# Fourier mixing spread over all four head pairs of a batch, with a third pair of row buffers, and work of the hand-over moved into the first MLP tile

## The chip, the cores and the metric

One core of a Trainium2 chip runs the whole program. The metric is the device time of one execution in microseconds, the median of the runs shown. The engines are named as the profile names them: PE (matmul), DVE (vector), ACT (scalar), POOL (GpSimd) and SP, whose queue issues most DMAs.

## The reference

Causal attention with a forgetting bias, then a block that mixes tokens and channels by a two-dimensional Fourier transform, then a layer norm and an MLP, with a residual. B is 8, H is 8, S is 576, D is 64; the MLP goes 512 to 2048 to 512. All in float32.

```python
cum = cumsum(maximum(s, 0), -1)
scores = q @ k.T / sqrt(D) + minimum(-(cum[:, None] - cum[None, :]), 0)   # causal
attn = softmax(scores);  x = (attn @ v) as (B, S, H * D)
u = x + real(fft(fft(x, axis=1), axis=2))
un = (u - mean(u)) / sqrt(var(u) + 1e-6)
out = u + maximum(un @ w_ch1, 0) @ w_ch2
```

## The kernel before, in words

**Head pairs.** The loop over `i` goes through 32 pairs of heads, four to a batch (pair `i` is head pair `j = i % 4` of batch `b = i // 4`). One pass weaves generators ("streams") of several pairs: `scores(i)` (matmuls L491 and L492 into the PSUM tile ps, exponential L495 on ACT into P), `av(i - 1)` (matmuls L523), `maxes(i + 1)` (matmuls L459 into pm, row maxima L462 and L466 on DVE into Mx, transposed by L471), the splitting of q and k into high and low parts (`high`, `low`: L418, L420 on ACT, L435 on DVE, L438 on POOL), `recip(i - 2)` (the softmax denominators: sums, L538 and L539 on DVE, then by DMA through rd to the broadcast rb) and `finish(i - 2)` (L559: the pair's rows of x into xa, or by way of xr and three DMAs into xs). `weave` always takes the next step of the stream that has the smallest share of its total behind it. A stream is given as a generator and a total; a larger total makes it slower.

**Order.** PE's instructions stand in the order in which the Python code traces them, up to the MLP (`manual_schedule`). On the other engines, on all DMA queues, and in the MLP also on PE, the scheduler of the tile framework orders instructions at build time by its own model of time; the order is fixed in the program.

**Mixing.** When a batch is complete, `folds(b)` turns its xa and xs (two tiles of 128 x 2 x 576 floats each) into even and odd sums: per half jj an addition Aw on DVE (L251) and a subtraction Bw on POOL (L253), then Df and the split into De (L256, L70), then Df and the split into Do (L260, L70), and at the end the row e and its parts eh (L263 to L266). A split is a rounding copy on ACT (L69) and a subtraction on DVE (L70). `fourier(b)` then runs two passes. The first has three sine pieces (six matmuls L284 into pzs) and three cosine pieces (seven matmuls L292, L294 into pzc), each split into zs or zc. The second has, for two column halves kc, nine matmuls L306 into pyc and nine L315 into pys, each in three slices, then ym and yp (L320, L321 on DVE), four additions into xa and xs on POOL (L322 to L325), and at the end the write of xa and xs to uD in DRAM. Every fourth batch ends with a matmul group L336 and L338, L339. ps, pyc, pys, pzs, pzc and the MLP's h share three PSUM banks (`bank`); pm and pav share five others.

`folds(b)` begins in pair 4b + 6, and `fourier(b)` is traced in pairs 4b + 8 on. How much of it each pair takes, and at which pace, is in the table `MIX`, by `i % 4`; the whole costs FOURIER (8900) in the units in which its steps yield.

**Weights.** The MLP's weights come as 64 bit floats and are made into float32 on the chip, in chunks of 256 columns: L83, ACT's L84, L85, L88, L87, then POOL's L89. `convert_w` does 24 chunks and writes them to wD in DRAM; `load_w` reads those back for feed-forward blocks f below 6 and does the other 40 chunks itself (`rounded` in it), and splits all into wh and wl (L112, L114).

**The hand-over.** In pair 31 the first token tile's layer norm begins (`ln_tile`: mean, then the centred uch and ucl, then the squares' sum, var, and r, the reciprocal root, L158 and L159). Then one weave finishes `av(31)`, batch 6's mixing, the norm and the first weights, `finish(31)` and the folds of batch 7 follow, and nine MLP tiles of 512 tokens begin (`mlp_tile`: sixteen blocks f of twelve matmuls L183 into h, zh on ACT L187, zl on DVE L188, twelve matmuls L196 to L198 into acc). Batch 7's mixing is woven into the first MLP tile; weights from f = 8 on are loaded into space that the mixing's tiles leave.

## Time and profile before

| what | value |
|---|---|
| median of 3 runs | 1428.15 us (1423.54 to 1430.72) |
| the profiled execution | 1426.1 us, span 1424.4 us |
| PE busy | 1305.1 us (92%) |
| DVE busy | 745.7 us (52%) |
| POOL, ACT busy | 561.6 us (39%), 539.3 us (38%) |
| granted TensorE clock, mean | 0.971 |

All times within the kernel are microseconds from the start of the span. A group or wait that is named by a line (L466) is that line of the code above. In a wait, the name behind the arrow is what came last. Matmuls overlap, so the time of one row is a latency; what a sequence costs is read from start to start. The head pairs last until 544 us, the first MLP matmul starts at 572.4 us, and the first MLP tile ends at about 697.6 us.

### The profile page before, as it was taken

What the parts mean: (1) busy time and instruction counts of PE and PEld (TensorE: products, weight loads), DVE (VectorE), ACT (ScalarE), POOL (GpSimd) and SP (SyncE); (2) the same over time, 40 slices, a digit from 0 to 9 for tenths busy, and PEclk for the clock granted to TensorE, in tenths of its full rate; (3) what the DMA queues carried; (4) which work ended last, traced back from release to release, by engine and by line L of the source; (5) the groups of instructions that cost most, each with busy time, mean ns of one, the idle gap of its engine ahead of it and who ended that gap; (6) DMA issues with size and microseconds to landing.
All of it is one profiled execution on the core that took longest, in us unless ns stands there. A gap on an engine that the chain in (4) does not pass through costs nothing.

```text
span 1424.4 us, 17997 instructions
## 1 busy us (share of the span) xinstructions
PE 1305.1 (92%) x6190; PEld 1068.7 (75%) x6190; DVE 745.7 (52%) x1684; ACT 539.3 (38%) x1211; POOL 561.6 (39%) x543
## 2 busy tenths in 40 slices
PE   4887979897988887997899999999999999999998
PEld 3766868686777676775688888888888888888886
DVE  6667677877777788799833233222332223322212
ACT  4775756676665656344321121211212112121110
POOL 6445465656546566565720402204022040123300
PEclk9998999999999997999899999999999999999999
DMA  8555556565655555433200000000000000000000
GB/s 214 156 159 144 163 149 180 158 168 159 159 161 144 166 149 163 162 123 121 79 8 30 31 30 15 15 30 31 30 15 15 30 30 30 15 16 0 30 0 30
DMA packets 78230, 125.05 MB, mean 88 GB/s; under 512 B 11256, under 2 KB 36249, under 8 KB 78139
## 3 DMA queue, kind: packets, MB, share of 16 engines
q1 hardware_dynamic: 75627, 119.83, 28.4%
q0 software_dynamic: 1696, 2.50, 0.9%
q10 hardware_dynamic: 816, 1.57, 0.3%
q8 instruction: 49, 0.80, 0.2%
q14 instruction: 42, 0.34, 0.1%
HBM read 76.85 MB, written 23.07 MB: 70 GB/s over the span
## 4 chain that ended last, share of the span: by engine, by line
PE 51%; DVE 7%; POOL 2%; DMA 1%; issue 1%; ACT 1%; SPq 0%; DVEq 0%; POOLq 0%; ACTq 0%
PE h L183 25%; PE acc L198 8%; PE acc L196 8%; PE acc L197 8%; POOL we L89 1%; DVE wm L88 1%; DVE we L83 1%; DVE wm L85 1%; DVE we L87 1%; DVE wl L114 1%; ACT wh L112 1%; DMA wl<-wD 0%; POOL wl L114 0%; DVE ucl L148 0%; DVE zl L188 0%
## 5 line engine op out<-in xcount | busy, mean ns | idle before, releaser
L188 DVE SCALAR_TENSOR_TENSOR zl<-h,zh 128x512 fp32r<-128x512 f32 x144 | 98.6, 686 | 405.5 <-ACT zh L187 405.4
L187 ACT ACTIVATE zh<-h 128x512 fp32r<-128x512 f32 x144 | 85.9, 596 | 530.1 <-PE h L183 530.1
L198 PE MATMUL acc<-zl,wh 128*128 128x512 f32 x576 | 227.5, 396 | 4.9 <-DVE zl L188 4.9
L196 PE MATMUL acc<-zh,wh 128*128 128x512 f32 x576 | 227.6, 395 | 1.0 <-ACT zh L187 1.0
L197 PE MATMUL acc<-zh,wl 128*128 128x512 f32 x576 | 226.8, 394 | 0.0
L523 PE MATMUL pavB<-P,va 128*128 128x320 f32 (+2 forms) x640 | 189.1, 389 | 9.5 <-ACT stage L527 8.9
L459 PE MATMUL pm<-KQ 128*128 128x256 f32 (+3 forms) x384 | 156.5, 427 | 44.4 <-DVE Mx L466 23.1
L495 ACT ACTIVATE P<-ps 128x320 f32<-128x320 f32 (+4 forms) x384 | 145.9, 393 | 110.5 <-PE ps L492 106.8
L491 PE MATMUL ps<-KQ 128*128 128x256 f32 (+2 forms) x384 | 154.1, 404 | 24.4 <-ACT P L495 14.0
L183 PE MATMUL h<-uch,wh 128*128 128x512 f32 x576 | 159.9, 398 | 8.3 <-ACT wh L112 8.3
L183 PE MATMUL h<-uch,wl 128*128 128x512 f32 x576 | 158.1, 396 | 0.8 <-DVE wl L114 0.8
L183 PE MATMUL h<-ucl,wh 128*128 128x512 f32 x576 | 156.9, 393 | 0.0
L466 DVE CUSTOM_DVE_ANT_0 trash<-pm,amask 128x128 bf16<-128x128 f32 (+3 forms) x256 | 123.5, 482 | 34.2 <-PE pm L459 16.9
L212 POOL TENSOR_TENSOR o<-o,w 128x512 f32<-128x512 f32 x32 | 41.8, 1305 | 252.3 <-issue 218.5
L183 PEld LDWEIGHTS h<-uch,wh 128*128 128x128 f32 x576 | 108.2, 190 | 35.9 <-ACT wh L112 12.1
L198 PEld LDWEIGHTS acc<-zl,wh 128*128 128x128 f32 x576 | 108.7, 189 | 32.0 <-DVE zl L188 6.9
L183 PEld LDWEIGHTS h<-uch,wl 128*128 128x128 f32 x576 | 109.2, 190 | 26.6 <-DVE wl L114 1.2
L196 PEld LDWEIGHTS acc<-zh,wh 128*128 128x128 f32 x576 | 108.6, 188 | 26.1 <-ACT zh L187 1.8
L183 PEld LDWEIGHTS h<-ucl,wh 128*128 128x128 f32 x576 | 108.9, 189 | 24.7
L197 PEld LDWEIGHTS acc<-zh,wl 128*128 128x128 f32 x576 | 108.6, 189 | 24.7
L459 PEld LDWEIGHTS pm<-KQ 128*128 128x128 f32 x384 | 78.4, 207 | 64.7 <-DVE Mx L466 30.2
L492 PE MATMUL ps<-q,k 128*128 128x256 f32 (+2 forms) x384 | 120.5, 316 | 3.1 <-POOL q L438 3.1
(140 smaller groups left out, 2066.9 us busy)
## 6 DMA issues: line engine op xcount, KB each, us to landing
qk<-in_qkT_dram SPq DMA_DIRECT2D x32, 576.0 KB
raw<-in_wP_dram SPq DMA_DIRECT2D x64, 256.0 KB
va<-in_vA_dram SPq DMA_DIRECT2D x32, 480.0 KB
q<-KQ SPq DMA_DIRECT2D x32, 288.0 KB
k<-KQ SPq DMA_DIRECT2D x32, 288.0 KB
rb<-rd SPq DMA_DIRECT2D x64, 144.0 KB
u<-uD SPq DMA_DIRECT2D x8, 1024.0 KB
out_dram<-o SPq DMA_DIRECT2D x32, 256.0 KB
```

Source lines behind the costliest of these rows:

```text
L183: nc.tensor.matmul(h[:, :n], a[:, j * 128:(j + 1) * 128], b[:, j, :n], start=i == 0, stop=i == 11)
L187: nc.scalar.activation(zh[:, :n], h[:, :n], AF.Relu)
L188: nc.vector.scalar_tensor_tensor(out=zl[:, :n], in0=h[:, :n], scalar=0.0, in1=zh[:, :n].bitcast(F32), op0=ALU.max, op1=ALU.subtract)
L196: nc.tensor.matmul(acc[j][:, :n], a[:, cs], y[:, :n], start=g == 0, stop=False)
L197: nc.tensor.matmul(acc[j][:, :n], b[:, cs], y[:, :n], start=False, stop=False)
L198: nc.tensor.matmul(acc[j][:, :n], a[:, cs], z[:, :n], start=False, stop=g == NF - 1)
L459: nc.tensor.matmul(p[:, :n], qy[:, h, 128 * c:128 * c + 128], ky[:, h, k0:k0 + n], start=True, stop=True)
L466: nc.vector.tensor_tensor_reduce(out=trash[:nq, :n], in0=p[:nq, :n], in1=amask[:nq, m0:m0 + n], scale=1.0, scalar=first if x else NEG, op0 ...
L491: nc.tensor.matmul(p[:, :n], ky[:, h, ksl], qy[:, h, a:a + n], start=True, stop=False)
L492: nc.tensor.matmul(p[:, :n], k1[:, h, ksl], q1[:, h, a:a + n], start=False, stop=True)
L495: nc.scalar.activation(P[:, o:o + a + n - lo], p[:, lo - a:n], AF.Exp, scale=0.125)
L523: nc.tensor.matmul(p[:, a - lo:n], va[:, c, vs], P[:, o:o + w], start=c == 0, stop=c == cs[-1])
```

## The change

`MIX` gives each of the four head pairs about a quarter of a batch's mixing (0.22, 0.26, 0.26 and the rest), where the first two had 0.3 each and the third took the rest. As mixing then reaches into the fourth pair, xa and xs get three buffers instead of two; the space comes from the descriptor area for POOL's DMAs, cut to 4096 bytes of a partition. The copy of row xs[0, 0] to x256 moves from the end of `folds` to the start of `fourier`. The folds are traced three steps in the third pair and four in the fourth, where it was five and two. The share of `convert_w` is 1.5 times as large in pairs 0 and 1 and half as large in pairs 2 and 3.

In the hand-over, batch 6's mixing stops after 4500 units, its first pass; its second pass and all of batch 7's mixing follow in the weave of the first MLP tile, and so does the rest of the first tile's norm (the squares' sum, var and r). For that, `ln_tile` allocates r and fills LN after its fourth centred block.

```diff
-    MIX = ((0.3, 0.25), (0.3, 0.4), (1, 0.35), (1, 0.05))
+    MIX = ((0.22, 0.22), (0.26, 0.26), (0.26, 0.26), (1, 0.26))
...
-            xbuf[b] = (fft.tile([128, 2, S], F32, tag="xa", name="xa", bufs=2), fft.tile([128, 2, S], F32, tag="xs", name="xs", bufs=2))
+            xbuf[b] = (fft.tile([128, 2, S], F32, tag="xa", name="xa", bufs=3), fft.tile([128, 2, S], F32, tag="xs", name="xs", bufs=3))
...
-            streams.append([later(take(folding, 5), 2), 7 / 0.7])
+            streams.append([later(take(folding, 3), 3), 6])
...
-            streams.append([folding, FOLDS - 5])
+            streams.append([folding, (FOLDS - 3) / 0.8])
...
-        share = NC1 * 4.0 / (NP - 2) if i < NP - 2 else (1.0, 4.0)[i - NP]
+        share = NC1 * 4.0 / (NP - 2) * (1.5, 1.5, 0.5, 0.5)[i % 4] if i < NP - 2 else (1.0, 4.0)[i - NP]
...
-    weave([later(call(recip, NP - 2), 2), 10], [later(call(finish, NP - 2), 4), 10], [av(NP - 1), AV], [mixing, FOURIER * 0.1], [norm, 6 * 0.4],
+    weave([later(call(recip, NP - 2), 2), 10], [later(call(finish, NP - 2), 4), 10], [av(NP - 1), AV], [take(mixing, 4500), FOURIER * 0.1],
...
-    mixing = fourier(b, *xbuf.pop(b))
+    mixing = chain(mixing, fourier(b, *xbuf.pop(b)))
...
-            streams.append([chain(idle(1000), mixing), FOURIER * 0.6])
+            streams.append([mixing, FOURIER * 0.9])
+            streams.append([later(norm, 1), 16])
...
-    nc = bacc.Bacc("TRN2", target_bir_lowering=False, num_devices=1)
+    nc = bacc.Bacc("TRN2", target_bir_lowering=False, num_devices=1, dynamic_dma_scratch_size=4096)
```

Three places of the order show it. The first is DVE where the third pair of a batch (pair 10) passes into the fourth (pair 11); L466 on Mx_128 is the first row maximum traced in pair 11, "L466 ISA Mx" reads its accumulator out, k is the low part of a later pair's keys. Before:

```order
L256 TENSOR_TENSOR Df<-Aw 128x289
L435 TENSOR_TENSOR k_2129<-qk,KQ_119 64x576 x2
L70 TENSOR_TENSOR De_1943<-Df,De_1942 128x289
L260 TENSOR_TENSOR Df<-Bw 128x288
L466 ISA trash,Mx_128<-pm,amask 128x128
L466 ISA Mx_128 128x1
L70 TENSOR_TENSOR Do_1945<-Df,Do_1944 128x288
L83 TENSOR_SCALAR we<-raw 128x256
L85 TENSOR_SCALAR wm<-raw 128x256
L88 SCALAR_TENSOR_TENSOR wm<-raw,wm 128x256
L87 SCALAR_TENSOR_TENSOR we<-raw,we 128x256
L466 ISA trash,Mx_128<-pm,amask 128x256
```

Now:

```order
L256 TENSOR_TENSOR Df<-Aw 128x289
L435 TENSOR_TENSOR k_2104<-qk,KQ_119 64x576 x2
L466 ISA trash,Mx_128<-pm,amask 128x128
L466 ISA Mx_128 128x1
L70 TENSOR_TENSOR De_2007<-Df,De_2006 128x289
L260 TENSOR_TENSOR Df<-Bw 128x288
L70 TENSOR_TENSOR Do_2009<-Df,Do_2008 128x288
L466 ISA trash,Mx_128<-pm,amask 128x256
L466 ISA Mx_128 128x1
L466 ISA trash,Mx_128<-pm,amask 128x384
```

One split De and one Df have moved behind the first maximum, and the chunk of weights behind the third.

The second is DVE in the first half of pair 10, at the softmax denominators (sums). Before:

```order
L466 ISA trash,Mx_129<-pm,amask 128x384
L466 ISA Mx_129 128x1
L320 TENSOR_TENSOR ym<-yc,pys 128x290
L321 TENSOR_TENSOR yp<-yc,pys 128x290
L466 ISA trash,Mx_129<-pm,amask 128x512
L466 ISA Mx_129 128x1
L462 TENSOR_REDUCE M_1895<-pm 64x1
L466 ISA trash,Mx_129<-pm,amask,M_1895 64x320
L466 ISA Mx_129 64x1
L538 TENSOR_SCALAR sums<-sums 32x36
```

Now:

```order
L466 ISA trash,Mx_129<-pm,amask 128x384
L466 ISA Mx_129 128x1
L466 ISA trash,Mx_129<-pm,amask 128x512
L466 ISA Mx_129 128x1
L538 TENSOR_SCALAR sums<-sums 32x36
L539 RECIPROCAL sums<-sums 32x36
L462 TENSOR_REDUCE M_1884<-pm 64x1
L466 ISA trash,Mx_129<-pm,amask,M_1884 64x320
```

The first half's ym and yp are gone from here, and sums stands two maxima earlier.

The third is SP's queue in the hand-over: rb is the broadcast of the last pairs' denominators, xs the rows of pairs 30 and 31, wD a chunk of converted weights, uD the mixed rows of batch 6. Before:

```order
L541 DMA rd<-sums 32x36
L98 DMA wD<-we 128x256
L544 DMA rb<-rd 64x576
L561 DMA xs<-xr 112x576
L562 DMA xs<-xr 15x576
L563 DMA xs<-xr 1x16x36
L328 DMA uD<-xs 128x576
L544 DMA rb<-rd 64x576
L327 DMA uD<-xa 128x2x576
L329 DMA uD<-xs 128x576
L561 DMA xs<-xr 112x576
```

Now:

```order
L541 DMA rd<-sums 32x36
L544 DMA rb<-rd 64x576
L561 DMA xs<-xr 112x576
L562 DMA xs<-xr 15x576
L563 DMA xs<-xr 1x16x36
L544 DMA rb<-rd 64x576
L561 DMA xs<-xr 112x576
```

The write of a chunk and the writes of batch 6's rows no longer stand among the broadcasts.

More of the change, by code (lines that the diff above doesn't have):

```diff
@@ L125, in spread_sum @@
         return m
+    LN, W = {}, {}
     def ln_tile(t0, n, lag):
@@ L149, in ln_tile @@
             nc.scalar.activation(uc, uc, AF.Square)
+            if j == 3:
+                r = mlp.tile([128, TOK], F32, tag="r", name="r")
+                LN[t0] = (uch, ucl, mu, r)
             yield 1.0
@@ L156, in ln_tile @@
         pv = spread_sum(t, "var", n)
-        r = mlp.tile([128, TOK], F32, tag="r", name="r")
         nc.scalar.activation(r[:, :n], pv[:, :n], AF.Sqrt, bias=eps)
         nc.vector.reciprocal(r[:, :n], r[:, :n])
-        LN[t0] = (uch, ucl, mu, r)
-    LN, W = {}, {}
     def mlp_tile(t0, n):
@@ L266, in folds @@
         nc.vector.tensor_sub(eh[32:33], e, eh[0:1].bitcast(F32))
-        nc.sync.dma_start(out=x256[b % ZB:b % ZB + 1], in_=xs[0:1, 0])
         folded[b] = (De, Do)
@@ L271, in fused_kernel @@
     FOLDS = 7
-    MIX = ((0.3, 0.25), (0.3, 0.4), (1, 0.35), (1, 0.05))
+    MIX = ((0.22, 0.22), (0.26, 0.26), (0.26, 0.26), (1, 0.26))
     def fourier(b, xa, xs):
         De, Do = folded.pop(b)
+        nc.sync.dma_start(out=x256[b % ZB:b % ZB + 1], in_=xs[0:1, 0])
         zc = [fft.tile([97, 3, 258], F32R, tag=f"zc{i}", name=f"zc{i}") for i in range(2)]
```

## Prediction

> **What bounds the kernel now.** I read the stages first (busy time by stretch, cut at the first matmul of head pair 8, the last score, the first MLP matmul, the end of the last batch's mixing and the end of the first MLP tile), because the share of the whole span mixes stages with different limits. Columns: length, busy us of PE, weight loads, DVE, ACT, POOL, then the granted TensorE clock, DMA share, GB/s.
>
> ```profile
> 142.80:544.00 401.20, 349.04 (x1995) 296.25 (x1994) 297.87 (x848) 253.53 (x635) 235.73 (x242) 0.96 0.57 160
> 544.00:572.40 28.40, 22.21 (x113) 18.97 (x112) 24.06 (x44) 18.01 (x39) 18.02 (x15) 0.76 0.53 159
> 572.40:620.60 48.20, 42.90 (x219) 34.73 (x218) 40.39 (x88) 19.42 (x44) 25.30 (x28) 1.00 0.41 139
> 620.60:697.60 77.00, 63.21 (x246) 46.87 (x244) 71.84 (x154) 36.07 (x80) 49.49 (x55) 0.95 0.32 108
> 697.60:1424.40 726.80, 721.15 (x3112) 586.24 (x3112) 212.79 (x277) 126.37 (x215) 157.47 (x117) 1.00 0.07 24
> ```
>
> The last row is PE at its limit and the change leaves its matmuls alone: nothing is to be had there. Before it PE stands idle for 52.2, 6.2, 5.3 and 13.8 us. In 620.6 to 697.6 the engine that has no room is DVE (71.84 of 77.00). The 52.2 us I then cut at the head pairs (pairs 20 to 27, from each pair's first score matmul to the next):
>
> ```profile
> 344.00:359.70 15.70, 14.84 (x94) 12.74 (x93) 11.12 (x38) 11.97 (x30) 8.32 (x10) 1.00 0.54 152
> 359.70:374.60 14.90, 14.53 (x90) 12.67 (x89) 8.91 (x31) 9.89 (x26) 5.84 (x6) 1.00 0.66 158
> 374.60:393.80 19.20, 16.11 (x98) 13.30 (x97) 17.82 (x44) 11.85 (x30) 15.50 (x16) 1.00 0.56 157
> 393.80:411.70 17.90, 13.77 (x73) 11.63 (x72) 12.99 (x38) 9.51 (x25) 8.88 (x11) 0.90 0.56 169
> 411.70:426.90 15.20, 14.52 (x93) 12.70 (x92) 10.20 (x35) 12.04 (x31) 6.35 (x9) 1.00 0.61 172
> 426.90:442.30 15.40, 14.17 (x90) 12.64 (x89) 9.61 (x34) 10.57 (x27) 9.84 (x10) 1.00 0.59 157
> 442.30:462.70 20.40, 16.24 (x88) 13.93 (x87) 16.84 (x41) 10.07 (x27) 13.73 (x13) 0.92 0.48 130
> 462.70:480.70 18.00, 13.71 (x71) 10.45 (x72) 13.12 (x36) 11.44 (x28) 9.89 (x12) 1.00 0.60 182
> ```
>
> The reader is to see a period of four. Call the pairs of a batch m0 to m3 (pair number modulo 4). m0 and m1 are PE's (idle 0.9, 0.4, 0.7, 1.2 us); m2, which holds the folds, is DVE's (17.82 of 19.20); in m2 and m3 PE is idle 3.1, 4.1, 4.2, 4.3 us. Who ends these waits, over the whole stretch, and how one border of m2 and m3 looks (pairs 10 and 11):
>
> ```profile
> PE pm L459 <- DVE Mx L466: 18.7, 9, 5.5
> PE ps L491 <- ACT P L495: 11.8, 14, 2.2
> ```
> ```profile
> 174.49 0.29 DVE L466 CUSTOM_DVE_ANT_0 trash<-pm,amask 128x128 bf16<-128x128 f32 x1
> ...
> 196.52 0.28 DVE L466 CUSTOM_DVE_ANT_0 trash<-pm,amask 128x128 bf16<-128x128 f32 x1
> ```
> ```profile
> 196.63 0.43 ACT L69 CAST Do<-Df 128x288 fp32r<-128x288 f32 x1 [3.18 <-DVE Df L260]
> ```
> ```profile
> 196.87 0.69 PE L459 MATMUL pm<-KQ 128*128 128x384 f32 x1 [4.30 <-DVE Mx L466]
> ```
>
> DVE takes 22.0 us from the first row maximum of m2 to the first of m3 and is busy nearly throughout; PE waits 4.30 us for that maximum, and ACT, behind a cast that needs a fold, 3.18 us. I call this maximum the gate: what shortens DVE's 22.0 us shortens the batch.
>
> **The change, part by part.** First, DVE between the two maxima of m2 and m3. By the order of instructions the changed kernel has one pair ym, yp (L320, L321) less there, since one half of the second pass now ends in m3, and one De split and one Df of L260 go behind the gate.
>
> ```profile
> L260 DVE TENSOR_TENSOR Df<-Bw 128x288 f32<-128x288 f32 x12 | 9.8, 819 | 0.5
> ...
> L70 DVE TENSOR_TENSOR De<-Df,De 128x289 fp32r<-128x289 f32 x12 | 7.3, 605 | 0.1
> ...
> L320 DVE TENSOR_TENSOR ym<-yc,pys 128x290 f32<-128x290 f32 x12 | 5.4, 452 | 0.1
> ```
>
> That is 2 x 0.45 (yp has ym's shape) + 0.61 + 0.82 = 2.3 us less. Everything else of the folds, both Aw included, still stands before the gate, because DVE's order takes them early though the code has half of them in m3. Against this stands a wait. With ym and yp gone from m2's first half, DVE comes to the denominators (sums, L538) 0.9 us sooner, in every batch in the same place, right behind the 512 wide maximum; when it came too soon before, it stood still, with the other maxima and so PE's pm behind it:
>
> ```profile
> 245.91 0.38 DVE L538 TENSOR_SCALAR sums<-sums 32x36 f32<-32x36 f32 x1 [1.30 <-DMA sums<-rows]
> ```
> ```profile
> 448.27 0.67 DVE L538 TENSOR_SCALAR sums<-sums 32x36 f32<-32x36 f32 x1 [2.67 <-DMA sums<-rows]
> ```
>
> The bounds are 0 (the other batches) and 2.7 us a batch; I take 1.3, the nearer row in position. So the gate comes 2.3 - 1.3 = 1.0 us earlier. Four of the eight POOL additions of the second pass leave m2 as well; POOL and DVE slow each other there:
>
> ```profile
> L251 DVE TENSOR_TENSOR Aw<-xa,xs x12: 737/934/1800, 183.0 to 524.7; 128x576 f32<-128x576 f32 x12
> ```
> ```profile
> L322 POOL TENSOR_TENSOR xa<-xa,ym x12: 788/815/1196, 178.2 to 532.5; 128x289 f32<-128x289 f32 x12
> ```
>
> 4 x 0.82 = 3.3 us of POOL leave the 15.50 of m2, a fifth. The two Aw lie 2 x (0.93 - 0.74) = 0.4 us above their shortest by the median and 2 x (1.80 - 0.74) = 2.1 by the longest; a fifth of something between is 0.3 us (bounds 0 and 2.1), since Bw and the q subtractions stay beside the folds.
> [...]
>
> Second, PE's share of mixing. A sine or cosine piece of the first pass and nine matmuls of the second take:
>
> ```profile
> 608.23 0.87 PE L284 MATMUL pzs<-dsin,Do 128*96 128x256 f32 x6
> 608.93 0.88 PE L292 MATMUL pzc<-dcos,De 128*96 128x258 f32 x6
> ...
> 615.77 1.37 PE L315 MATMUL pys<-ssin,zs 96*128 96x290 f32 x9
> 616.98 1.37 PE L306 MATMUL pyc<-scos,zc 97*128 97x290 f32 x9
> ```
>
> From start to start 0.70 and about 0.84 for the pieces, 1.21 for nine, so 0.40 for a slice of three. By the quotas m0 goes from two pzs and two pzc to two and one (-0.84), m1 from one of each and four slices to one pzs and two pzc (-0.76), m2 from eight slices to seven, m3 from none to five (+2.0). m0 and m1 are PE's: -1.6 at full value. m3 after the gate is PE's too (13.77 + 4.1 makes the pair): +2.0 at full value. m2's slice lies beside DVE's work: 0.
> Sum a batch: -1.0 - 0.3 - 1.6 + 2.0 = -0.9 us; batches 0 to 5 run in head pairs 8 to 31: 6 x -0.9 = -5 us. For PE's clock another 2 us: 0.96 over 401 us is 16 us of full clock lost, and I give an eighth back. The convert_w share and the folds' paces are in these counts: m1, m2 and m3 hold one chunk of weights each, m0 none. The third pair of row buffers costs no instruction; it takes away POOL's wait for an earlier batch's write to uD, and no release of PE's waits is of that kind. The x256 copy moves on SP's queue from the folds to m0, 2 KB, behind the qk load; hidden. The descriptor space serves only the nine table loads on POOL's queue, which stand where they stood: 0.
>
> Third, the tail. PE no longer runs the second pass of batch 6 and the var sum before the first h; it enters the MLP right behind the last pzc. The reciprocal of r leaves this chain:
>
> ```profile
> 562.68 3.28 DVE L159 RECIPROCAL r<-r 128x512 f32<-128x512 f32 x1
> ```
> ```profile
> 562.78 0.34 SPq L541 DMA_DIRECT2D rd<-sums  x1
> 568.53 0.34 SPq L98 DMA_DIRECT2D wD<-we  x1
> ...
> 574.33 0.49 SPq L544 DMA_DIRECT2D rb<-rd  x1
> ```
> ```profile
> 577.46 0.76 DVE L559 TENSOR_TENSOR xr<-stage,rb 128x576 f32<-128x576 f32 x1 [3.05 <-DMA rb<-rd]
> ```
>
> Behind it stood a weight chunk (L87), its product on POOL, its write on SP (568.53), and behind that the broadcast rb of the last pair, for which DVE waits at 577.46. With r, that write and the uD write gone from ahead of rb, the last folds start some 4 us earlier (0, if POOL's xr of pair 30 still holds SP, to 11.5, all from 562.78 to 574.33). But 620.6 to 697.6 is DVE's, and there the work grows:
>
> ```profile
> L87 DVE SCALAR_TENSOR_TENSOR we<-raw,we 128x256 int32<-128x256 int32 x29 | 16.4, 571 | 0.4 <-ACT we L84 0.2
> L88 DVE SCALAR_TENSOR_TENSOR wm<-raw,wm 128x256 f32<-128x256 uint16 x29 | 16.2, 559 | 0.6
> L85 DVE TENSOR_SCALAR wm<-raw 128x256 int32<-128x256 int32 x29 | 12.7, 437 | 0.0
> L83 DVE TENSOR_SCALAR we<-raw 128x256 int32<-128x256 int32 x29 | 12.2, 424 | 0.0
> ```
>
> A chunk of weights is these four, 1.99 us; by the order 32 stand there instead of the 29 of these rows (+6.0), and r (+3.3): 9.3 us more. Ahead of it stand fewer: one chunk instead of four before the first zl, eight instead of eleven to thirteen from there to the end of mixing, and no r. Work only moved comes out at 0; but of 44 chunks behind the last maximum 42 are left, the other two are done in the head pairs, and their 4.0 us are the gain, less 1 us of new idling of DVE, which now has little to do until PE's third h: -3 us. Bounds: -12 (the 11.5 and all of the clock at 0.76) and +9 (the stretch starts no earlier).
>
> Sum against the profiled execution's own time, 1426.1 us: -5 - 2 - 3 gives 1416; the median of the three runs, 1428.15, lies 2 above that execution, so 1418 by the median; 1417 is my value.
>
> **Rivals.** The balance works as its numbers intend: m2 and m3 fall to the idle time of m0 and m1. From the rows (3.1 + 4.1 + 4.2 + 4.3) / 2 - 1.6 = 6.3 us a batch, 38 over six: 1390. Against it: the folds are not spread on DVE. Chance 0.08.
> The four additions held the folds up for their whole length: 3.3 instead of 0.3 us a batch, 18 over six: 1399. The 1800 ns of L251 speak for it; against it, the two Aw have only 2.1 us to give. [...] Chance 0.08.
> The clock stays full. Halves of the clock follow long PE waits; the 4.3 us wait becomes about 3.3. If that is below what the clock tolerates, most of the 16 us comes back: 1404. For it, pairs 20 to 22 ran at 1.00 with 0.9, 0.4 and 3.1 us idle; against it, pair 27 ran at 1.00 with 4.3 us idle, so idle time alone doesn't set it. [...] Chance 0.10.
> The change does not do what it says: DVE's wait for sums eats the 2.3 us whole, m3's slices cost PE what m0 and m1 save, and the tail hands back at DVE what it gains at SP: 1426 to 1430. Chance 0.20.
> Slower: banks. Scores, pyc and pys share three PSUM banks. At the end of m2 the order now opens the second pyc while the first pys still waits for yp, which DVE reaches only behind the folds; one bank is left for scores, and each of the four score groups there costs a matmul pair, an exponential and both handovers, about 1.0 us instead of 0.3 (the 11.8 us in 14 waits above are 0.8 each): +2.8 a batch, 17 over six, and no gain at the gate (+6): 1440. It decides from about 1.5 us a batch. Chance 0.14.
>
> **How the numbers follow.** My forecast has 0.40, and its own range is 1408 to 1426. Slower by 0.5% begins at 1435, faster at 1421; less than that a measurement of this kernel can't tell from no change. Faster: 0.32 of the forecast, and the three rivals of 0.08, 0.08 and 0.10, 0.58. Same: 0.08 + 0.20 = 0.28. Slower: 0.14. The range from 1396 to 1437 leaves out the full balance and the worse half of the banks.
>
> **What would show it.** Right: m0 and m1 together 1.6 us shorter (30.6 in both batches above), m2 and m3 together 0.7 longer (37.1 and 38.4), PE's wait for Mx at the m3 border near 3 us, a DVE wait for sums of 1 to 2 us in each m2; xr about 4 us sooner behind the last score; the stretch from the end of batch 7's mixing to the end of the first MLP tile near 85 us instead of 77. Wrong: PE's wait for Mx gone (balance), or waits of ps for yp and P above 1.5 us a batch (banks), or the first tile ending later behind the last score than 153.6 us (544.0 to 697.6).

## The result, and the profile after

The changed kernel takes 1463.05 us (median of 4 runs, 1458.45 to 1463.91) against 1427.28 us before on the same chip (1423.54 to 1430.72): ratio 1.0245, interval 1.0210 to 1.0279. It is 36 us slower where 10 us less was forecast. The profiled execution has a span of 1460.7 us; before it was 1424.4.

The stages, cut at the same events as before (first score of pair 8, last score, first h, end of batch 7's mixing, first h of the second MLP tile). Columns as in the prediction. First after:

```profile
144.90:562.40 417.50, 364.21 (x1998) 307.16 (x1997) 317.54 (x857) 257.84 (x642) 236.58 (x242) 0.93 0.55 156
562.40:575.30 12.90, 11.22 (x73) 9.74 (x73) 9.65 (x17) 9.11 (x23) 9.31 (x10) 1.00 0.46 154
575.30:635.20 59.90, 51.24 (x254) 42.60 (x253) 44.14 (x88) 20.30 (x47) 31.50 (x32) 0.91 0.35 119
635.20:736.70 101.50, 72.88 (x261) 51.14 (x260) 85.71 (x174) 41.83 (x87) 56.84 (x61) 0.90 0.30 99
736.70:1460.70 724.00, 717.74 (x3101) 582.90 (x3099) 209.27 (x270) 124.97 (x213) 147.29 (x112) 1.00 0.07 23
```

and the last two rows of before, cut at the second tile (702.5) instead of the end of the first:

```profile
620.60:702.50 81.90, 68.09 (x258) 50.71 (x257) 76.20 (x160) 36.71 (x81) 52.24 (x57) 0.92 0.33 112
702.50:1424.40 721.90, 716.27 (x3102) 582.40 (x3100) 208.42 (x272) 125.73 (x213) 154.73 (x115) 1.00 0.06 23
```

The 36.3 us lie in four places: 2.1 in the first eight pairs (144.9 against 142.8), 16.0 in pairs 8 to 31 (417.5 against 401.5), 16.1 between the last score and the second MLP tile (562.4 to 736.7 is 174.3; 544.3 to 702.5 was 158.2), 2.1 behind that. Within the third place PE reaches the first h 15 us sooner (12.9 us behind the last score instead of 28), and loses twice that in the two stretches behind it.

Pairs 20 to 27 after, the pairs that the prediction showed:

```profile
355.50:370.40 14.90, 14.26 (x87) 12.09 (x86) 9.35 (x32) 10.49 (x27) 4.95 (x9) 1.00 0.81 235
370.40:386.80 16.40, 14.16 (x82) 11.71 (x82) 12.99 (x38) 11.39 (x28) 10.49 (x10) 1.00 0.57 165
386.80:408.00 21.20, 17.32 (x86) 14.31 (x87) 17.67 (x43) 12.39 (x31) 12.38 (x12) 0.87 0.49 143
408.00:425.80 17.80, 16.14 (x93) 13.37 (x93) 14.08 (x38) 9.30 (x24) 13.26 (x16) 0.96 0.41 123
425.80:440.10 14.30, 14.16 (x88) 11.96 (x86) 9.12 (x32) 10.20 (x26) 3.69 (x6) 1.00 0.71 219
440.10:456.80 16.70, 15.11 (x83) 12.92 (x83) 12.07 (x38) 11.30 (x29) 10.67 (x11) 0.90 0.62 163
456.80:477.20 20.40, 16.62 (x89) 13.59 (x88) 17.44 (x42) 12.27 (x32) 11.78 (x12) 0.93 0.54 148
477.20:494.40 17.20, 14.85 (x84) 12.34 (x84) 13.87 (x37) 9.65 (x26) 12.62 (x14) 0.99 0.39 107
```

PE's matmuls went where the quotas send them (m0 from 93 or 94 to 87 or 88, m3 from 71 or 73 to 84 or 93), but m1, from which work was taken, is longer (16.4 and 16.7 instead of 14.9 and 15.4). What ended PE's waits in pairs 8 to 31 (us in total, times, longest; before it was 18.7 for Mx and 11.8 for P):

```profile
PE ps L491 <- ACT P L495: 27.2, 21, 2.6
PE ps L492 <- POOL q L438: 10.7, 6, 2.0
PE pm L459 <- DVE Mx L466: 6.0, 11, 2.3
```

The wait that the change aims at, for the row maxima, is down by two thirds; waits for P and for POOL's q stand in its place. PE's idle time is the same, 53.3 us of 417.5 against 52.2 of 401.5; what grew is its busy time, and most of that is the clock (0.93 instead of 0.96, about 10 us). How little of these 10 us belongs to the change is told at the step "clock" below.

### The profile page after: what moved, and what is told of

It is laid out like the page before. It is cut to its first block, busy times and chain, and to the rows that moved or that the text cites. A ratio compares the mean times of both kernels' runs of the same rounds, so it can differ in the third digit from the quotient of the medians.

```text
span 1460.7 us, 17972 instructions
## 1 busy us (share of the span) xinstructions
PE 1324.6 (91%) x6190; PEld 1079.0 (74%) x6190; DVE 767.3 (53%) x1684; ACT 540.3 (37%) x1211; POOL 558.3 (38%) x543
## 4 chain that ended last, share of the span: by engine, by line
PE 64%; DVE 16%; DMA 8%; ACT 4%; issue 4%; POOL 3%; SPq 1%; DVEq 0%; POOLq 0%; ACTq 0%
PE h L183 25%; PE acc L198 8%; PE acc L196 8%; PE acc L197 8%; PE pavB L523 4%; PE pm L459 3%; DMA qk<-in_qkT_dram 3%; PE ps L491 2%; PE ps L492 2%; DVE k L435 2%; DVE wm L85 2%; DVE we L87 1%; DVE we L83 1%; DMA sums<-rows 1%; PE pavA L523 1%
## 5 line engine op out<-in xcount | busy, mean ns | idle before, releaser
L187 ACT ACTIVATE zh<-h 128x512 fp32r<-128x512 f32 x144 | 85.7, 596 | 533.4 <-PE h L183 533.4
L491 PE MATMUL ps<-KQ 128*128 128x256 f32 (+2 forms) x384 | 153.4, 401 | 38.7 <-ACT P L495 29.9
L459 PE MATMUL pm<-KQ 128*128 128x256 f32 (+3 forms) x384 | 159.7, 439 | 30.8 <-DVE Mx L466 13.6
L495 ACT ACTIVATE P<-ps 128x320 f32<-128x320 f32 (+4 forms) x384 | 144.0, 392 | 95.4 <-PE ps L492 92.2
L183 PE MATMUL h<-uch,wl 128*128 128x512 f32 x576 | 158.2, 397 | 1.5 <-DVE wl L114 1.5
L466 DVE CUSTOM_DVE_ANT_0 trash<-pm,amask 128x128 bf16<-128x128 f32 (+3 forms) x256 | 123.7, 483 | 27.5 <-PE pm L459 7.3
L183 PEld LDWEIGHTS h<-uch,wh 128*128 128x128 f32 x576 | 109.0, 192 | 37.9 <-ACT wh L112 14.5
L492 PE MATMUL ps<-q,k 128*128 128x256 f32 (+2 forms) x384 | 122.4, 321 | 12.2 <-POOL q L438 12.2
L198 PEld LDWEIGHTS acc<-zl,wh 128*128 128x128 f32 x576 | 109.5, 190 | 29.1 <-DVE zl L188 3.6
L183 PEld LDWEIGHTS h<-uch,wl 128*128 128x128 f32 x576 | 109.0, 190 | 27.9 <-DVE wl L114 2.8
L197 PEld LDWEIGHTS acc<-zh,wl 128*128 128x128 f32 x576 | 109.5, 190 | 25.1 <-POOL wl L114 0.5
L183 PEld LDWEIGHTS h<-ucl,wh 128*128 128x128 f32 x576 | 109.0, 189 | 24.8
L491 PEld LDWEIGHTS ps<-KQ 128*128 128x128 f32 x384 | 77.7, 202 | 63.0 <-ACT P L495 40.5
```

Source lines behind the costliest of these rows:

```text
L183: nc.tensor.matmul(h[:, :n], a[:, j * 128:(j + 1) * 128], b[:, j, :n], start=i == 0, stop=i == 11)
L187: nc.scalar.activation(zh[:, :n], h[:, :n], AF.Relu)
L197: nc.tensor.matmul(acc[j][:, :n], b[:, cs], y[:, :n], start=False, stop=False)
L198: nc.tensor.matmul(acc[j][:, :n], a[:, cs], z[:, :n], start=False, stop=g == NF - 1)
L459: nc.tensor.matmul(p[:, :n], qy[:, h, 128 * c:128 * c + 128], ky[:, h, k0:k0 + n], start=True, stop=True)
L466: nc.vector.tensor_tensor_reduce(out=trash[:nq, :n], in0=p[:nq, :n], in1=amask[:nq, m0:m0 + n], scale=1.0, scalar=first if x else NEG, op0 ...
```

## The experiments

Before, after and the eighteen experiments at a glance. Ratio: to the kernel before on the same chip. m0 to m3: us of pairs 8 to 31, by pair number modulo 4, over six batches, from first score to first score. Late: from the last score to the second MLP tile. Chunks: chunks of weights converted behind the end of mixing. All but the ratio come from one profiled execution; kernels with the same order in the pairs differ there by up to 3.6 us. On all five engines, tail, tail_mix, tail_norm and norm_sooner have the order of before in pairs 8 to 30, and heads, heads_space and space that of after. Their means are 402.9 us (five kernels, 401.5 to 404.8) and 415.7 us (four, 413.9 to 417.5): the change costs the pairs 13 us rather than the 16 of the two single profiles.

| kernel | ratio (interval) | pairs 8-31 | m0, m1, m2, m3 | late | chunks |
|---|---|---|---|---|---|
| before | 1 | 401.5 | 95.0, 89.7, 108.2, 108.6 | 158.2 | 29 |
| after | 1.0245 (1.0210 to 1.0279) | 417.5 | 87.7, 100.6, 122.3, 106.9 | 174.3 | 32 |
| heads | 1.0177 (1.0150 to 1.0205) | 413.9 | 86.9, 100.4, 121.2, 105.5 | 170.7 | 32 |
| tail | 1.0125 (1.0095 to 1.0154) | 404.8 | 96.2, 92.4, 111.2, 105.0 | 171.6 | 29 |
| bufs_only | 1.0170 (1.0137 to 1.0202) | 410.3 | 93.4, 94.2, 113.0, 109.7 | 176.5 | 32 |
| heads_space | 1.0064 (1.0043 to 1.0085) | 417.5 | 86.4, 101.3, 123.4, 106.4 | 153.3 | 29 |
| space | 1.0198 (1.0164 to 1.0232) | 413.9 | 86.7, 101.2, 119.5, 106.5 | 173.6 | 31 |
| x256_only | 1.0053 (1.0029 to 1.0077) | 413.0 | 96.3, 95.9, 108.0, 112.8 | 157.1 | 29 |
| low_early | 1.0259 (1.0231 to 1.0286) | 416.0 | 109.9, 85.7, 111.3, 109.1 | 177.2 | 32 |
| hs_defer | 1.0079 (1.0051 to 1.0107) | 418.4 | 86.2, 92.8, 120.7, 118.6 | 157.9 | 29 |
| no_folds | 1.0161 (1.0131 to 1.0191) | 408.7 | 87.7, 102.1, 123.4, 95.6 | 175.2 | 32 |
| hs_nofolds | 1.0002 (0.9983 to 1.0020) | 409.6 | 87.8, 101.1, 122.1, 98.6 | 155.9 | 29 |
| hs_nofolds_defer | 1.0039 (1.0018 to 1.0061) | 413.5 | 87.4, 92.2, 121.1, 112.8 | 154.7 | 29 |
| folds_only | 1.0067 (1.0044 to 1.0090) | 406.2 | 95.9, 89.2, 108.8, 112.3 | 167.2 | 31 |
| no_share | 1.0361 (1.0338 to 1.0385) | 427.6 | 89.8, 106.5, 104.7, 126.6 | 184.8 | 32 |
| mix_space | 1.0107 (1.0068 to 1.0146) | 420.7 | 88.0, 105.4, 109.5, 117.8 | 155.7 | 29 |
| share_only | 1.0068 (1.0042 to 1.0094) | 409.8 | 96.6, 90.9, 119.2, 103.1 | 155.8 | 29 |
| tail_mix | 1.0036 (1.0018 to 1.0054) | 402.1 | 91.5, 92.5, 109.0, 109.1 | 163.0 | 31 |
| tail_norm | 1.0129 (1.0084 to 1.0173) | 402.9 | 93.9, 89.5, 109.5, 110.0 | 173.6 | 31 |
| norm_sooner | 1.0073 (1.0051 to 1.0096) | 403.2 | 94.1, 91.3, 114.5, 103.3 | 169.3 | 32 |

**The two halves, heads and tail.** "heads" is after with the hand-over of before; "tail" is before with these lines as in after, the other way round.

```diff
-    ... [take(mixing, 4500), FOURIER * 0.1],
+    ... [mixing, FOURIER * 0.1], [norm, 6 * 0.4],
-    mixing = chain(mixing, fourier(b, *xbuf.pop(b)))
+    mixing = fourier(b, *xbuf.pop(b))
-            streams.append([mixing, FOURIER * 0.9])
-            streams.append([later(norm, 1), 16])
+            streams.append([chain(idle(1000), mixing), FOURIER * 0.6])
```

> The change in the head pairs alone (MIX, third row buffers, the x256 copy, folds three and four, the chunk share 1.5 and 0.5); the hand-over is that of before. Theory: the loss has two separate halves, and the head pairs hold 18 us of it (last score 562 instead of 544 us): 1427 + 18 = 1445 us, with the wait of PE for POOL's q in every pair m1 and the clock near 0.93. Rival: the head pairs are late only because of something that the hand-over also needs (row buffers, POOL's descriptor space), and the loss is not additive: near 1463 or near 1427.

> The change in the hand-over alone (batch 6's second pass and the first tile's norm in the MLP); the head pairs are those of before. Theory: the hand-over holds 16 us: 1427 + 16 = 1443 us, the first h some 15 us sooner behind the last score and the second tile some 16 us later. Rival: the hand-over of before would lose as much behind the new head pairs, because those leave other work (42 chunks instead of 44) to it: then this kernel is at 1427 or below, 1424 by the prediction's third term.

Measured: +26.7 and +18.1 us, together 45 where the whole loses 36. The halves overlap: "heads" keeps the old hand-over and yet loses 12.5 us between the last score and the second tile, with 32 chunks of weights behind the end of mixing instead of 29. Something in the head pairs' half reaches into the MLP.

**The third row buffers' space: bufs_only, heads_space, space.** bufs_only puts bufs=3, the smaller descriptor space and the x256 copy's new place into before. The other two take the third buffer from attb, the pool that closes before the MLP:

```diff
+        xpool, n = (attb, 1) if b % 3 == 2 else (fft, 2)
-        xbuf[b] = (fft.tile(... tag="xa", bufs=3), fft.tile(... tag="xs", bufs=3))
+        xbuf[b] = (xpool.tile(... tag="xa", bufs=n), xpool.tile(... tag="xs", bufs=n))
```

> Before, with nothing but the third pair of row buffers (and the smaller descriptor space and the x256 copy that go with it). Theory: the buffers' 9.2 KB of a partition push the weights that the first MLP tile converts into space that batch 7's mixing still holds, so that by the order 8 instead of 11 chunks stand ahead of the end of mixing and 32 behind it: the head pairs stay at 544 us, the stretch from the end of mixing to the second tile grows from 83 to 99 us, 1430 + 16 = 1446 us. Rival: an unused buffer costs nothing, the 16 us of the heads-only kernel come from MIX: 1430.

> The heads-only kernel, with the third pair of row buffers taken from the pool that closes before the MLP (batches 2 and 5 use it), so that the MLP's space is as before. Theory (space): the stretch from the end of mixing to the second tile comes back from 99 to 83 us, 1456 - 16 = 1440 us, and the 17 us of the head pairs stay. Rival (MIX leaves the late stretch slower by itself): 1456.

> After, with the same move of the third buffers. By the order 10 instead of 8 chunks stand ahead of the end of mixing. Theory: of the stretch's 102.5 us the part that the tail-only kernel does not show (93.3) goes, 9 us, and up to 4 us for the two chunks counted twice by the clock: 1463 - 9 = 1454 us (1450 to 1456). Rival: the late stretch is set by the norm's place alone: 1463.

Measured: 1456, 1440 and 1459 us. The last stretch before the second tile, in bufs_only and then in heads_space:

```profile
631.80:731.10 99.30, 75.24 (x267) 53.06 (x265) 82.92 (x173) 39.25 (x84) 57.23 (x62) 0.88 0.31 101
```
```profile
634.50:716.30 81.80, 68.75 (x266) 51.28 (x264) 76.52 (x161) 36.73 (x82) 52.18 (x58) 0.92 0.32 106
```

99.3 us with the buffers in fft, 81.8 with the same buffers elsewhere. The loads of weights on SP's queue show why. Those of before ahead of the end of mixing and those of bufs_only:

```profile
583.63 36.58 SPq L78 DMA_DIRECT2D raw<-in_wP_dram  x14
```
```profile
593.64 19.04 SPq L78 DMA_DIRECT2D raw<-in_wP_dram  x6
637.45 7.52 SPq L78 DMA_DIRECT2D raw<-in_wP_dram  x5
```

Fourteen loads in a row before; in bufs_only eight (two stand in a row ahead), and the next only at 637.45, behind the last write of mixing's rows (636.65): their buffers now lie in space that mixing still holds. The trace does not name that wait; that the loads come early again in heads_space, with the buffers elsewhere, is what speaks for it. DVE then stands still, and starts its chunks late; after shows it too:

```profile
644.02 0.29 DVE L83 TENSOR_SCALAR we<-raw 128x256 int32<-128x256 int32 x1 [4.50 <-DMA raw<-in_wP_dram]
```

So the space costs some 16 us with the old hand-over. With the new one (space) the late part gains next to nothing, 173.6 us instead of 174.3, and the expected 1454 us were missed. The late part of the four kernels with after's pairs makes a table of two by two: 153.3 us with neither cost (heads_space), 170.7 with the buffers alone (heads), 173.6 with the new hand-over alone (space), 174.3 with both (after). Each costs 17 to 20 us alone, and the second adds little, since by then the stretch is held up already; for the hand-over it is mostly the moved norm (below). And bufs_only loses 9 us in the head pairs, which was not expected of it.

**SP's queue and POOL's q: x256_only, low_early, hs_defer, hs_nofolds_defer.** x256_only moves in before nothing but this line; low_early traces the low parts sooner in after; the two deferred kernels (hs_defer from heads_space, hs_nofolds_defer from hs_nofolds) issue the writes to uD (of batches 0, 1, 2, 4 and 5) ahead of the next batch's second pass, and the x256 copy ahead of its own batch's.

```diff
-    nc.sync.dma_start(out=x256[b % ZB:b % ZB + 1], in_=xs[0:1, 0])
     folded[b] = (De, Do)
...
 def fourier(b, xa, xs):
     De, Do = folded.pop(b)
+    nc.sync.dma_start(out=x256[b % ZB:b % ZB + 1], in_=xs[0:1, 0])
```
```diff
-    streams.append([later(low(i + 1), i % 4 == 0), (6, 7, 4, 3)[i % 4]])
+    streams.append([low(i + 1), (8, 7, 4, 3)[i % 4]])
```
```diff
-    nc.sync.dma_start(out=uD[0:2, :, ts]...); uD[2, :, ts]; uD[3, :, ts]
+    unwritten.append(write) if b in (0, 1, 2, 4, 5) else write()
 ...
     for x in range(2): ...   # z256
+    nc.sync.dma_start(out=x256[b % ZB:b % ZB + 1], in_=xs[0:1, 0])
+    while unwritten: unwritten.pop()()
     for kc in range(2): ...
```

> After, with the low parts of q and k traced earlier in m0, so that POOL's q stands between m0's two P instead of behind both in pairs 16 and 20. Theory: PE's wait of 2.0 us for q in m1 and the 3.4 us at half clock behind it (1.7 us) go in four to six batches: m1 16.8 to 15.0 us, 4 to 6 x 1.8 = 7 to 11 us less, 1452 to 1456. Rival: PE only reaches the next wait (DVE is at 13 us of 16.8 in m1, so the row maxima end it): 1463 within 3 us.

> Before, with nothing but the x256 copy moved from the end of the folds to the start of the mixing; two row buffers, old MIX. Theory (queue): the 2 KB copy now stands on SP's queue ahead of the load that feeds POOL's q, so the scheduler places q behind m0's second P in every batch (by the order), PE waits for it in m1: the head pairs hold the 9 us that the buffers-only kernel lost there, the late stretch stays at 83 us: 1430 + 9 = 1439 us. Rival: those 9 us come from the buffers or are a chance of the clock: 1430 to 1433.

> The kernel with the head pairs' change and the buffers' space as before (1439.9), and now the writes to uD of batches 0, 1, 2, 4 and 5 and the x256 copy are issued later, ahead of the next batch's second pass in m1. By the order POOL's first q then stands ahead of m0's second P in four of six batches. Theory (queue): the wait for q goes there, and the clock's halves behind it; 4 to 5 x 1.8 = 7 to 9 us less, 1431 to 1433 us, m1 near 15 us. Rival (next wait): PE meets the row of maxima (KQ by mt) or P instead, as with the low parts traced earlier: 1437 to 1440.

> The same, and the uD writes and the x256 copy issued later as in the deferred kernel, so that POOL's q comes sooner in m0. Theory (next wait): m1 falls by 8 us over six batches as it did there, and m3 gives it back as there: 1431 to 1435. Rival (queue): what m3 gave back there was the folds' casts; without them the 8 us stay, 1423 us, and this beats the kernel before.

The chain in after, pair 28 (m0) into pair 29: SP's queue, then POOL, then PE.

```profile
493.72 0.54 SPq L327 DMA_DIRECT2D uD<-xa  x1
494.31 0.47 SPq L328 DMA_DIRECT2D uD<-xs  x1
494.87 1.01 SPq L329 DMA_DIRECT2D uD<-xs  x1
...
499.37 0.58 SPq L276 DMA_DIRECT2D rows<-xs  x1
500.00 0.58 SPq L98 DMA_DIRECT2D wD<-we  x1
500.63 0.69 SPq L430 DMA_DIRECT2D q<-KQ  x1
```
```profile
508.17 0.63 POOL L498 TENSOR_SCALAR_AFFINE_SELECT P<-P 128x512 f32<-128x512 f32 x1 [6.13 <-ACT P L495]
509.12 0.40 POOL L501 TENSOR_SCALAR_AFFINE_SELECT P<-P 128x64 f32<-128x64 f32 x1 [0.31 <-ACT P L495]
509.60 3.21 POOL L438 TENSOR_TENSOR q<-qk,q 64x576 fp32r<-64x576 f32 x2
```
```profile
511.44 0.39 PE L492 MATMUL ps<-q,k 128*128 128x256 f32 x1 [2.04 <-POOL q L438]
```

Ahead of q's load (L430) stand three writes of a batch, which used to start some 4 us into m3 and now stand at its end, and the x256 copy (rows<-xs). My reading is that the scheduler, by its own model of time, then expects q's load later; what the trace shows is that it puts POOL's q behind m0's second P, in all six m0. On the chip POOL stands idle for 6.13 us ahead of that P, and PE waits 2.04 us for q. The 2 KB copy is enough: before has its first q ahead of the second P in four of six m0, x256_only in none, and it loses 7.4 us (1437.0), as expected. In its trace only 1.4 us more are booked as waits for q (3.9 instead of 2.5 us); m1 is 6.2 us longer and m3 4.2. The wait is one symptom among others. In low_early it is gone, and PE waits for the row of maxima instead (KQ<-mt, 13.4 us in 4 waits): m1 falls by 15 us, m0 grows by 22 (1466 us). In hs_defer q's wait falls from 10.6 to 1.8 us and m1 by 8.5, as forecast, and m3 grows by 12.2; PE now waits 18.2 us in 12 waits for ACT's stage copies (1443 us, later than both forecasts). Without the folds' split (hs_nofolds_defer) it is the same: m1 -8.9, m3 +14.2, slower by 7.6 us than hs_nofolds (1438 us, again later than both). The "next wait" won three times in kind, and twice cost more than forecast. Which reordering makes m3 longer there was not taken apart.

**The folds' split: no_folds, folds_only, hs_nofolds.**

```diff
-    streams.append([later(take(folding, 3), 3), 6])
+    streams.append([later(take(folding, 5), 2), 7 / 0.7])
...
-    streams.append([folding, (FOLDS - 3) / 0.8])
+    streams.append([folding, FOLDS - 5])
```

in after (no_folds) and in heads_space (hs_nofolds); folds_only is the reverse edit in before.

> After, with the folds traced five and two as before. By the order only 17 instructions of DVE and ACT move. Theory: the waits for P in m3 (1.5 us each), where ACT's cast Do stands ahead of an exponential, belong to the folds that went behind the first maximum: without the new split they shrink, 0 to 6 us less, 1460 us. Rival: the order is nearly the same, 1463 within 2 us.

> Old hand-over, MIX, the chunk share and three row buffers (the third taken from the pool that closes before the MLP), folds traced five and two as before. Theory: the folds' new split costs about 9 us in m3 (ACT's cast Do ahead of an exponential), with any hand-over: 1440 - 9 = 1431 us, m3 near 96 us over six batches instead of 106. Rival: it did so only beside the new hand-over: 1440.

> Before, with the folds traced three and four alone. Theory: ACT's cast Do goes behind the first maximum and ahead of an exponential also without MIX: 4 to 9 us more, 1435 to 1440. Rival: the old MIX has no slices of mixing and few scores waiting in m3, so that the casts cost nothing there, and the gate's 0.6 and 0.8 us come back as the prediction has it: 1424 to 1431.

Measured: no_folds takes 1454 us, a larger gain than forecast, and has m3 at 95.6 instead of 106.9, the pairs at 408.7 instead of 417.5; hs_nofolds takes 1430 us, 0.6% less than heads_space; folds_only loses 0.67% alone (4.7 us in the pairs, little more than kernels of one order differ by; the rest late, where a different order leaves 31 chunks). What the split does in after, pair 23, on ACT and PE:

```profile
411.20 0.43 ACT L69 CAST Do<-Df 128x288 fp32r<-128x288 f32 x1 [3.24 <-DVE Df L260]
411.65 0.71 ACT L495 ACTIVATE P<-ps 128x256 f32<-128x256 f32 x2
...
412.09 0.47 PE L491 MATMUL ps<-KQ 128*128 128x448 f32 x1 [1.45 <-ACT P L495]
```

The fold that went behind the first maximum took its cast along. ACT waits 3.24 us for DVE's Df, the exponentials behind the cast wait with it, and the scores wait for them. A row like it stood in the prediction too (3.18 us), as a reason to expect a gain. The length of these waits hardly moves (ACT's for Df in pairs 8 to 31: 25.5 us before, 29.9 after, 28.7 in no_folds); what the edit changes is what stands behind them. In m3 PE's waits for P are 1.5 us before, 9.4 after and 4.2 in no_folds. In m2 they are 9.3, 16.5 and 16.2: that growth is not the split's.

**The chunk share: no_share, mix_space, share_only.**

```diff
-    share = NC1 * 4.0 / (NP - 2) * (1.5, 1.5, 0.5, 0.5)[i % 4] if ...
+    share = NC1 * 4.0 / (NP - 2) if ...
```

in after (no_share) and in hs_nofolds (mix_space); share_only is before with the uneven share.

> After, with the even chunk share of before. Theory: m1's loss is POOL's q, which stands behind both of m0's P in POOL's order with or without the share: 1463 less 0 to 4, 1460 us, the wait for q stays in most m1. Rival: the loss of m1 is the chunk of weights that the share puts there (DVE 13 us instead of 9.5): then m1 comes back to 15 us, 6 x 1.8 = 11 us less, 1452.

> MIX and the x256 copy alone, three row buffers without their cost in space, even chunk share, old folds, old hand-over. Theory: the share 1.5 and 0.5 is worth 10 to 16 us to the new MIX (after without it was that much slower), so this is at 1441 to 1447 us, with long waits for Mx in m3. Rival: the share matters only beside the new folds: 1431.

> Before, with the chunk share 1.5 and 0.5 alone. Theory: it was worth 11 us in the head pairs to the new MIX (417.5 against 427.6 us with the even share), since no chunk of weights stands in m3 any more; here m3 loses its chunk too (by the order) and POOL's q stands ahead of m0's second P in every batch: 0.3 to 1% less than before, 1417 to 1427 us, and the one part of the change that gains. Rival: with the old MIX m3 ends in the wait for Mx, which the chunk stands behind: 1430 within 4.

With MIX the uneven share is worth 15 to 18 us (no_share against after, mix_space against hs_nofolds; 10 or 11 us of it in the pairs): PE waits 20.0 us for Mx in no_share, three times some 6 us at the first maximum of m3, and 6.0 in after. It is not the chunk that PE waits for: a chunk begins 7.8 us into pair 11 in both, behind that maximum; ahead of it stand, in no_share, a De and a Df of the folds (196.50 to 198.40). So the share acts by the order that it makes the scheduler choose. In m2 it costs time in all three comparisons (122.3 against 104.7 us, 122.1 against 109.5, 119.2 against 108.2); why was not taken apart. The first expectation was a miss, both theories. Alone it loses 8.5 us: m2 grows by 11, m3 shrinks by 5.5. So it is not the part that gains by itself, as the theory had it.

**The hand-over's parts: tail_mix, tail_norm, norm_sooner.** tail_mix takes the two lines on mixing of the tail's diff, tail_norm those on norm (with r and LN allocated sooner), and norm_sooner writes [later(norm, 1), 34] for 16.

> Before, with batch 6's second pass moved into the first MLP tile, the norm left in its old place. Theory: the hand-over's loss is the norm of the first tile (r, 3.3 us, and the squares' sum on a DVE that has no room there); moving the mixing alone gives PE back what it takes: 1430 to 1433 us. Rival: the loss is the mixing, which keeps the weights' space 14 us longer: 1440 to 1448.

> Before, with the first tile's var and r moved into the MLP, and the mixing in its old place. Theory: this is the part of the hand-over that loses, 12 of its 18 us (the tail kernel at 1448 less the mixing's 1436): 1441 to 1443 us, with the last chunk of weights one zl later. Rival: the two parts lose only together: 1431 to 1434.

> The kernel with only the norm moved into the MLP, with its total 34 instead of 16, so that by the order r stands behind the fifth block's zl, ahead of the end of mixing, and not behind the ninth. Theory: r and its squares' sum cost because they stand where DVE has no room: 4 to 5 us less than the norm's kernel, 1.0095 of before, 1443 us. Rival: what costs is that the norm leaves the weights' chunks fewer places ahead of the end of mixing (31 behind it in both): 1450.

Measured: mixing +5 us, norm +18 to 20, against +18 for both. The norm's place is worth 8 of them: behind the fifth zl instead of the ninth, ahead of the end of mixing, where DVE waits for PE's last matmuls, it costs 10.5. There are 32 chunks behind the end of mixing then and not 31, so it is not the number of chunks that decides. About 10 us stay with the norm in the sooner of the two places; that part was not taken apart.

**A version that beats both?** None. hs_nofolds (MIX, the share and the buffers, without the folds' split, the new hand-over and the cost in space) equals before: 1.0002, interval 0.9983 to 1.0020. So the new quotas with the share, and with all that they do to the order, neither gain nor lose. Its profile has the pairs 8 us longer than the profile of before, and the late part 2 us shorter; of the medians on one chip (1430.34 and 1431.00) nothing of that is to be seen, so the single rows of the table are not to be read closer than some 5 us.

## Why the prediction was wrong, step by step

By the ratios, which rest on several runs each, the loss adds up so: MIX with the share, the x256 copy and a third pair of buffers costs nothing (hs_nofolds, 1.0002); the folds' split makes it 1.0064 (heads_space), 9 us; the new hand-over and the buffers in the MLP's space make it 1.0245 (after), 26 us. So two steps of the prediction failed above all: the hand-over with the buffers, put at -3 and 0 us, and the folds moved behind the gate, booked as a gain. The -5 us of the pairs did not come either, and the steps below say why.

The pairs can be summed from the table, each row adding one part: before 401.5; with the x256 copy moved and three buffers 410.3 (bufs_only); with MIX 420.7 (mix_space); with the share 409.6 (hs_nofolds); with the folds' split 417.5 (heads_space): +8.8, +10.4, -11.1, +7.9, together the 16.0 of after (13 by the means above). Single steps are good to 2 to 4 us, and between bufs_only and mix_space the buffers' place changes too.

- **Step "the gate" (-1.0 us a batch).** The spacing of the two first maxima was to go from 22.0 to 21.0 us. It went, in the mean of five borders, from 21.9 to 22.4. The wait for sums is there in every one of six batches with 1.5 to 2.7 us, mean 2.06, but before already had some: over the five borders it grew from 0.9 to 2.2, by the 1.3 that the prediction took. What failed is the 2.3 us of work: DVE's busy time between the two maxima fell by 0.9 alone (19.77 to 18.90). One pair ym and yp, one De and one Df of L260 are gone from there, as booked; the two Df of L256 that stay take 1.2 us more, the first of them beside POOL's q subtraction (the next step). With the folds traced as before (no_folds) the spacing is the same, 22.4. PE's wait for Mx shrank all the same (18.7 to 6.0 us), but neither the quotas nor the share do that alone: with the even share it is 20.0 us (no_share), with the old quotas 25.1 (share_only). What failed beside it is the idea that m2 and m3 end at DVE's gate alone: ACT's queue, with the casts of the folds ahead of the exponentials, takes over at once. The fold moved behind the gate was booked as 0.61 + 0.82 us gained; it costs some 8 to 9.
- **Step "contention" (-0.3).** The two Aw gave back 0.3 us a batch, as forecast (13.0 us over six batches to 11.3; median 934 to 748 ns). The Df of L256 took 0.9 a batch more, which outweighs it. Pairs 8 to 31, before and then after, and one place of after:

```profile
L256 DVE TENSOR_TENSOR Df<-Aw 128x289 f32<-128x289 f32 x12 | 8.7, 728 | 0.1
```
```profile
L256 DVE TENSOR_TENSOR Df<-Aw 128x289 f32<-128x289 f32 x12 | 13.9, 1158 | 0.0
```
```profile
187.12 1.69 DVE L256 TENSOR_TENSOR Df<-Aw 128x289 f32<-128x289 f32 x1
```
```profile
186.91 3.16 POOL L438 TENSOR_TENSOR q<-qk,q 64x576 fp32r<-64x576 f32 x2
```

  In five of six batches the first Df stands so beside POOL's q and takes 1.68 to 1.69 us; the shortest takes 0.44. Two first Df of before began beside a q as well (at 185.98 and 387.01) and took 0.44; what makes the difference was not taken apart. The step counted what leaves POOL in m2, and not where POOL's other work goes in the new order.
- **Step "PE's share".** m0 fell by 1.2 us a batch (forecast 0.84). m1 was to lose 0.76 and gained 1.8. The line that failed is "the x256 copy moves on SP's queue ... hidden": it was costed by its bytes, and its price is the order that it makes the scheduler choose, 7.4 us alone. The uD writes, which move to the end of m3 with the second pass, were not costed at all; their part was not separated from the copy's. The order of POOL, where q stands behind the second P in every m0, does not appear in the prediction. m2, put at 0, grew by 2.4, which comes with the chunk share in all three comparisons above; m3, put at +2.0, fell by 0.3. The prediction has the share "in these counts", at no price of its own.
- **Step "clock" (-2).** No gain is to be seen. In pairs 8 to 31 the clock was at half for 34 us before and for 55 us after, 10 us lost more in these two executions. But the five traces with before's order in the pairs lost 17.1 to 23.9 us to the clock (before the least, mean 21.5), and the four with after's 18.8 to 27.3 (after the most, mean 21.8). So the 10 us are no more than kernels of one order differ by, and a lasting gain or loss of the clock in the pairs is not shown.
- **Step "the third pair of row buffers costs no instruction", 0 us.** 16 us with the old hand-over; beside the new one, as in the change itself, 4 us (space against after, 7 by the ratios, whose intervals touch). It costs space, and the space is what the MLP's weights are loaded into.
- **Step "the tail" (-3).** With the buffers' space the largest miss: 26 us by the ratios, for the two together. The mixing of batch 7 ends 3.5 us sooner behind the last score, as forecast (4). DVE's work in the stretch behind it grows by 9.5 us (76.20 to 85.71), as forecast (9.3). But its idle time grows from 5.7 to 15.8 us (forecast 1): no raw weights at hand, an order with the norm in the wrong place. And the 4.0 us for two chunks less are not to be seen: DVE is busy for 44.14 of the 59.90 us up to the end of mixing, so it has room there. Which engine sets that end was not tested. The prediction's own two signs, 4 us sooner and a stretch 8 us longer, do not add up to -3.
- **The rivals.** "Banks" had the right symptom and the right size (waits for P above 1.5 us a batch: 15.4 us more over six, 2.6 a batch) and, for the pairs, the right time; the rows show another mechanism for part of it, an exponential behind a cast, and the folds' edit confirms that: it takes 5.5 to 8.7 us of these waits away (27.2 to 21.7 in no_folds, 29.6 in heads_space to 20.9 in hs_nofolds). 9 or 10 us of them, most in m2, stay with the old folds; whether the banks hold those was not tested. "No net change" and the three faster rivals are out. No rival was about the order that an edit without instructions brings, or about space.

The words ahead of the prediction say that a larger total makes a stream slower. It is the other way round: progress is counted as steps over total, so a larger total makes it sooner. No term rested on it.

## What to carry to other kernels

Where a scheduler decides the order, an edit has two prices: its instructions, and the order that it causes elsewhere. Read the order on every engine that waits or is waited for, also behind edits that seem free (a 2 KB copy moved on a queue cost 7.4 us here, 9 KB of buffers 16 beside the old hand-over), and check what the freed or taken space was used for next. A wait that is the largest of its kind is not the limit if the next engine's queue stands right behind it: the waits for Mx and for q, each time that they were taken away here, came back in another place. And a single profile of each kernel can mislead about the clock: several kernels that share a stretch show how far its loss varies by itself (17.1 to 23.9 us here, in five kernels with one order in the pairs).

## What the hardware did that was not expected

In these two traces the clock drops by whole windows of 3.41 us. In each of the two traces, before and after, all stretches at half clock lie on one grid and are one, two, three or four windows long (but for the last, at the end of the span). Three neighbouring windows of after, around the wait for q at 511.44 (PE busy is the first number behind the length):

```profile
508.39:511.80 3.41, 1.37 (x12) 1.17 (x11) 3.23 (x9) 2.31 (x6) 3.02 (x4) 1.00 0.29 87
511.80:515.21 3.41, 3.41 (x12) 2.87 (x11) 3.38 (x9) 1.95 (x6) 2.33 (x3) 0.50 0.85 213
515.21:518.62 3.41, 3.41 (x23) 3.05 (x23) 2.83 (x11) 1.48 (x4) 2.53 (x3) 1.00 0.38 108
```

PE was idle for 2.04 us of one window, and the whole next window ran at half, though PE was busy in all of it. Over both traces, before and after, from 142 to 722 us, a window at full clock with 2.0 us or more of idle time was always followed by a half one (18 of 18), one with 1.5 to 2.0 in 9 of 16 cases, one with 1.25 to 1.5 in 1 of 13, one with less in none of 251. So I put the price of a wait of 2 us that does not straddle two windows at up to 1.7 us more behind it, an estimate: half of 3.41. Several short waits in one window add up: 0.93, 0.11 and 0.80 us in the one from 655.2 of after brought a half window too. It fits that idle time of nearly the same total (53.3 and 52.2 us) lost 27 us of clock after and 17 before, and that kernels with one order in the pairs differ so much; my reading is that it matters where a wait falls on the grid. None of the windows around q's wait is idle as a whole: 2.04 us of 3.41, 60%, were enough.

In after, the chunks' price goes with what POOL does beside them. In the late stretch of after, two instructions of DVE of one kind and size, and POOL's product:

```profile
672.93 0.28 DVE L83 TENSOR_SCALAR we<-raw 128x256 int32<-128x256 int32 x1
673.13 0.83 DVE L85 TENSOR_SCALAR wm<-raw 128x256 int32<-128x256 int32 x1
```
```profile
673.09 0.72 POOL L89 TENSOR_TENSOR we<-wm,we 128x256 f32<-128x256 f32 x1 [0.36 <-DVE we L87]
```

The first takes 0.28 us; the second begins 0.04 us after the product has begun and takes 0.83, until 0.15 us after the product has ended. Over all of after, the 25 instructions of L85 with no work of POOL beside them take 0.28 to 0.29 us each. Of the 39 others, with POOL at work beside them, 29 take 0.81 to 1.51 us and ten 0.28 to 0.32. The prediction had looked for POOL and DVE slowing each other at the folds alone.
